# Spreading an attention kernel's PV and q matmuls over column tiles of the PE array

## The chip, the cores and the metric

The kernel runs on one core of a Trainium2 chip. The metric is the time of one execution on the device in microseconds (us). PE is the matmul engine (TensorE), DVE the vector engine, ACT the scalar engine, POOL the general one, SP the engine that issues the loads here. PE has a clock of its own. It is granted at full or at half rate and at nothing between (matmuls of 512 columns in a row start 216 or 427 ns apart); "clock" below means this granted rate, 1.00 being full.

## The reference

Two independent problems, A and B, each one decode step of sliding-window attention; the outputs are concatenated. Cut to what matters:

```python
B, Sq, D = 2, 1, 576;  Hq, Hkv, Sk, Dh = 32, 16, 16384, 128
W = min(4096, max(256, Sk // 4))                 # 4096: only the last W keys count
q = (x @ wq).reshape(B, Sq, Hq, Dh).transpose(0, 2, 1, 3)
k = repeat(k_cache[:, :, Sk - W:, :], 2, axis=1) # two query heads share a kv head
v = repeat(v_cache[:, :, Sk - W:, :], 2, axis=1)
p = softmax(einsum("bhqd,bhkd->bhqk", q, k) * Dh ** -0.5)
o = einsum("bhqk,bhkd->bhqd", p, v)
out = o.transpose(0, 2, 1, 3).reshape(B, Sq, Hq * Dh) @ wo   # all bf16
```

There is one query row per head and 134.2 MB of k and v to read, so arithmetic per byte is small. With wq and wo, 153.1 MB are read.

## The kernel before

The work comes in 32 slabs (16 kv heads of A, then of B), four slabs to a group, eight groups. A slab is 2 MB (2048 KB) of k and as much of v, for both batches. PV is the product of the probabilities and v. The loads go through one DMA queue into a ring of eight 2 MB slots, always in the same order: k of slab t, then v of slab t-5, and once per group a piece of wo.

For each slab DVE transposes k in two halves, and PE computes scores of both query heads and both batches. For each group a softmax chain follows: maximum (DVE), two tiny PE jobs, exponentials (ACT), a transpose of the probabilities (DVE), sums, reciprocals. Then PV. Slab m of a group owns 32 of the 128 PSUM partitions, which is one column tile of the PE array, and its 16 matmuls run one behind the other:

```python
ot = OTB[32 * m:32 * m + 32, :]
for j in range(j0, j1, 4):          # ... j0, j1 = 0, 64; the last slab in two parts
    z, bk, jj = j // 32, (j % 32) // 16, j % 16
    col = 512 * bk + 64 * (4 * z + m) + 4 * jj
    last = e.matmul(ot, pT[:, v, col:col + 32], ring[:, r, j * 128:(j + 4) * 128],
                    start=(j == 0), stop=(j == KR - 4), skip_group_check=True)
```

When all four slabs of a group are done, ACT evicts the bank, four matmuls with a selection matrix collect the wanted rows, DVE multiplies by the reciprocal sums, and eight matmuls, a mask and a reduction lay the heads out for the projection:

```python
evac_op[G] = [S.add("act", lambda e: e.activation(oE[:, :], OTB[:, :], ACTF.Copy), ...)]   # oE is fp32
for c in range(4):
    last = e.matmul(bank[:, 0:16], oE[:, 128 * c:128 * c + 128], selv[:, c, :], ...)
# ... norm (DVE), then
for j in range(8):
    last = e.matmul(bank[:, 16 * j:16 * j + 16], spread[:, j, :], oTg[...], start=True, stop=True)
# ... mask (DVE), reduce (DVE), then 16 projection matmuls into two column tiles
```

The q stage runs 36 matmuls per problem, each into one column tile (the same for all 36) of four different banks.

## Time and profile before

| | before |
|---|---|
| median of the first three executions | 379.18 us (377.11 to 382.23) |
| the traced execution | 382.22 us, of which the trace spans 380.5 us |
| PE busy | 309.3 us, 81% of the span |
| last load landed | 363.7 us after the span's start |
| last PV matmul ended | 372.7 us |

The busy row of the slices on the profile page (40 equal slices of the span, busy share in tenths; PEclk is the granted clock; DMA the busy share of the 16 DMA engines), kernel before:

```profile
PE   0778995998969876995969876797969976996895
PEclk9999898899889998999889988899689989897697
DMA  8999999999999999999999999999999999999900
```

PE looks almost full, but the row that never dips is DMA. It stops two slices before the end. The table by stretches shows where (columns: stretch in us, its length, then busy us and instruction count of PE, PEld (weight loads), DVE, ACT, POOL; then clock, DMA share, GB/s), kernel before:

```profile
350.00:355.00 5.00, 5.00 (x14) 1.84 (x13) 0.86 (x3) 0.00 (x0) 0.00 (x0) 0.55 1.00 427
362.00:364.00 2.00, 2.00 (x22) 1.09 (x22) 0.00 (x0) 0.00 (x0) 0.00 (x0) 1.00 0.11 43
364.00:366.00 2.00, 2.00 (x15) 0.97 (x11) 0.00 (x0) 0.00 (x0) 0.00 (x0) 1.00 0.00 0
```

Nothing moves after 364 us, yet the kernel goes on for 16 us. The trace also holds each landing of a load: most 2 MB slabs land 4.9 us after the one before, the last v slab at 360.3 us, its cut-off end at 360.9, the last two pieces of wo at 363.0 and 363.7.

What PE does in that time is seen in the timeline (start, duration, engine, line, operation, output and inputs, count; times in us), kernel before:

```profile
341.49 3.63 PE L537 MATMUL ot<-ring,pT 128*32 128x512 bf16 x16
349.60 6.05 PE L537 MATMUL ot<-ring,pT 128*32 128x512 bf16 x16
358.38 4.65 PE L537 MATMUL ot<-ring,pT 128*32 128x512 bf16 x14
...
364.35 8.40 PE L537 MATMUL ot<-ring,pT 128*32 128x512 bf16 x46
372.78 0.60 ACT L549 ACTIVATE oE<-ot 128x512 f32<-128x512 f32 x1 [16.10 <-PE ot L537]
373.43 1.06 PE L554 MATMUL tb<-selv,oE 128*128 128x16 f32 x8 [0.69 <-ACT oE L549]
374.53 0.17 DVE L561 TENSOR_TENSOR oTg<-tb,rsb 128x16 bf16<-128x16 f32 x1 [15.44 <-PE tb L554]
374.76 0.36 PE L575 MATMUL tb<-oTg,spread 128*128 128x16 bf16 x8 [0.27 <-DVE oTg L561]
...
375.83 2.08 PE L601 MATMUL pj<-wob,oP 128*2 128x288 bf16 x16 [0.71 <-DVE oP L587]
```

The first line is PV of slab 26 at full clock (3.6 us), the second PV of slab 27 at mostly half clock (6.1 us), and the line with x46 is nearly all of slabs 29 to 31. When the last v piece landed (360.9 us) PE was still in slab 28. So the end of this kernel is a queue of PE work behind loads that are already there.

### The profile page before, as it was taken

The page shows a single profiled execution, that of the slowest core. Times are in us where ns is not written, and L with a number is a line of the kernel's source. Part 1 is how long each engine was busy: PE and PEld are TensorE (multiplying, and loading weights), DVE is VectorE, ACT ScalarE, POOL GpSimd, SP SyncE. Part 2 cuts the span into 40 slices and gives each one's busy share as a digit, 9 for nine tenths or more (in the row PEclk, how much of TensorE's full clock was granted, in tenths as well). Part 3 has the DMA queues.
Part 4 walks back from the last instruction along what each step waited for, and adds up shares of the span by engine and source line. Part 5 has one row for each costly group of instructions (what it writes and reads, how often), then busy time and mean ns, then how long its engine had stood idle before and what let it go on. Part 6 is the DMA issues. An engine that isn't in the chain of part 4 may idle for free.

```text
span 380.5 us, 3541 instructions
## 1 busy us (share of the span) xinstructions
PE 309.3 (81%) x1500; PEld 133.4 (35%) x1500; DVE 184.4 (48%) x191; ACT 30.7 (8%) x104; POOL 15.5 (4%) x50
## 2 busy tenths in 40 slices
PE   0778995998969876995969876797969976996895
PEld 0433432343334333442424333243334423442442
DVE  3006596746464473447474473465475364543001
ACT  1022002001200020002000020001100020002001
POOL 6001000000000000000000000000000000000000
PEclk9999898899889998999889988899689989897697
DMA  8999999999999999999999999999999999999900
GB/s 334 434 414 432 431 427 422 432 427 427 425 424 431 424 429 431 425 429 420 434 424 434 422 425 434 422 429 423 429 432 424 432 427 422 428 431 425 382 19 3
DMA packets 10976, 153.34 MB, mean 403 GB/s; under 512 B 1224, under 2 KB 1232, under 8 KB 1616
## 3 DMA queue, kind: packets, MB, share of 16 engines
q1 hardware_dynamic: 10948, 153.10, 94.9%
q8 instruction: 12, 0.20, 0.2%
q14 instruction: 4, 0.03, 0.0%
q10 hardware_dynamic: 12, 0.01, 0.0%
HBM read 153.10 MB, written 0.00 MB: 402 GB/s over the span
## 4 chain that ended last, share of the span: by engine, by line
PE 51%; DMA 31%; DVE 14%; ACT 2%; issue 2%; DVEq 0%
PE ot L537 20%; DMA ring<-in_B_k_cache_dram 18%; PE st_0 L432 11%; DVE xt L409 11%; PE st_1 L432 10%; DMA ring<-in_A_k_cache_dram 9%; DMA ring<-in_A_wq_dram 4%; PE pj L601 2%; PE st_0 L262 1%; PE tb L554 1%; PE pj L262 1%; PE ot L262 1%; PE st_1 L262 1%; ACT qrow L271 1%; DVE nM L456 1%
## 5 line engine op out<-in xcount | busy, mean ns | idle before, releaser
L409 DVE STREAM_TRANSPOSE xt<-ring 128x2048 f32<-128x2048 f32 x64 | 144.5, 2284 | 88.7 <-DMA ring<-in_A_k_cache_dram 51.0
L432 PE MATMUL st_0<-xt,zq 128*128 128x512 bf16 x256 | 108.4, 424 | 38.1 <-DVE xt L409 38.0
L537 PE MATMUL ot<-ring,pT 128*32 128x512 bf16 x512 | 123.2, 401 | 0.0
L432 PE MATMUL st_1<-xt,zq 128*128 128x512 bf16 x256 | 108.2, 423 | 0.0
L537 PEld LDWEIGHTS ot<-ring,pT 128*32 128x32 bf16 x512 | 48.9, 101 | 73.8 <-issue 26.5
L432 PEld LDWEIGHTS st_0<-xt,zq 128*128 128x128 bf16 x256 | 26.3, 103 | 80.3 <-DVE xt L409 43.9
L432 PEld LDWEIGHTS st_1<-xt,zq 128*128 128x128 bf16 x256 | 26.7, 104 | 31.7 <-issue 10.5
L561 DVE TENSOR_TENSOR oTg<-tb,rsb 128x16 bf16<-128x16 f32 x8 | 1.4, 174 | 47.7 <-PE tb L554 47.7
L396 POOL TENSOR_TENSOR zq<-qs,bmask 128x64 bf16<-128x64 bf16 x32 | 9.2, 292 | 284.5 <-PE st_1 L432 251.2
L475 ACT ACTIVATE bias_sb<-tb 128x2 f32<-128x2 f32 x8 | 1.4, 172 | 228.2 <-PE tb L471 228.2
L601 PE MATMUL pj<-wob,oP 128*2 128x288 bf16 x128 | 14.6, 304 | 0.7 <-DVE oP L587 0.7
L244 PE MATMUL tb<-ident_b,xt 2*128 2x2 bf16 x36 | 2.3, 194 | 10.0 <-DVE xt L214 10.0
L501 DVE STREAM_TRANSPOSE pT<-pR 128x512 bf16<-128x512 bf16 x16 | 10.4, 686 | 0.0
L471 PE MATMUL tb<-ones_f,nMrep 1*128 1x1 f32 x32 | 4.8, 250 | 6.1 <-DVE nMrep L465 6.1
L456 DVE TENSOR_REDUCE nM<-tb 1x8 f32<-1x64 f32 x16 | 2.7, 207 | 14.0 <-PE tb L447 14.0
L262 PE MATMUL st_0<-ring,xU 128*32 128x512 bf16 x18 | 7.8, 434 | 2.1 <-DMA ring<-in_A_wq_dram 2.1
L554 PEld LDWEIGHTS tb<-selv,oE 128*128 128x128 f32 x64 | 8.2, 191 | 2.9 <-ACT oE L549 2.0
L554 PE MATMUL tb<-selv,oE 128*128 128x16 f32 x64 | 7.9, 255 | 1.4 <-ACT oE L549 1.4
L601 PEld LDWEIGHTS pj<-wob,oP 128*2 128x2 bf16 x128 | 6.7, 86 | 4.8 <-DVE oP L587 0.8
L482 ACT ACTIVATE pR<-st_0,bias_sb 128x256 bf16<-128x256 f32 x16 | 8.2, 543 | 0.3
L482 ACT ACTIVATE pR<-st_1,bias_sb 128x256 bf16<-128x256 f32 x16 | 8.2, 550 | 0.0
L441 DVE TENSOR_REDUCE mx<-st_0 128x2 f32<-128x512 f32 x8 | 5.3, 657 | 5.6 <-PE st_1 L432 5.6
(62 smaller groups left out, 109.3 us busy)
## 6 DMA issues: line engine op xcount, KB each, us to landing
ring<-in_A_k_cache_dram SPq DMA_DIRECT2D x16, 2048.0 KB, 32.1
ring<-in_A_v_cache_dram SPq DMA_DIRECT2D x16, 2048.0 KB, 32.8
ring<-in_B_k_cache_dram SPq DMA_DIRECT2D x16, 2048.0 KB, 34.1
ring<-in_B_v_cache_dram SPq DMA_DIRECT2D x15, 2048.0 KB, 29.9
ring<-in_A_wq_dram SPq DMA_DIRECT2D x1, 4608.0 KB, 13.6
ring<-in_B_wq_dram SPq DMA_DIRECT2D x1, 4608.0 KB, 24.1
wob<-in_A_wo_dram SPq DMA_DIRECT2D x4, 1152.0 KB, 26.2
wob<-in_B_wo_dram SPq DMA_DIRECT2D x3, 1152.0 KB, 25.3
```

Of the source, the lines that this page charges most:

```text
L262: last = e.matmul(QB[c][32 * P:32 * P + 32, :], xU[:, P, u, 0:32], wqv[P][:, u, c * 512:(c + 1) * 512], start=(u == 0), stop=(u == NU - 1) ...
L396: return e.tensor_tensor(dst, src, msk, ALU.mult)
L409: Xop[(t, jb)] = S.add("dve", lambda e: e.transpose(xt[:, n % NXT, :].bitcast(FP32), ring[:, r, jb * HW_:(jb + 1) * HW_].bitcast(FP32)), d ...
L432: last = e.matmul(st[bk][:, 0:512], zq[:, p4, m, 16 - 16 * jb:144 - 16 * jb], mv, start=(m == 0 and jb == 0 and p4 == 0), stop=True, skip_ ...
L441: mxs = [S.add("dve", lambda e, jb=jb: e.tensor_reduce(mx[:, jb, :], st[jb][:, :].rearrange("p (x t) -> p t x", t=2), AX.X, ALU.max), [Sop ...
L456: last = e.tensor_reduce(dst, src, AX.X, ALU.max, negate=True)
L471: last = e.matmul(bank[:, t:t + 1], nMrep[0:1, t, :], ones_f[0:1, 0:1], start=True, stop=True)
L482: last = e.activation(pR[:, jb, :].rearrange("p (x t) -> p t x", t=2)[:, t, :], st[jb][:, :].rearrange("p (x t) -> p t x", t=2)[:, t, :], ...
L501: chain[(G, "pT%d" % jb)] = S.add("dve", lambda e, jb=jb: e.transpose(pT[:, v, 512 * jb:512 * jb + 512].rearrange("p (w j q) -> p j w q", ...
L537: last = e.matmul(ot, pT[:, v, col:col + 32], ring[:, r, j * 128:(j + 4) * 128], start=(j == 0), stop=(j == KR - 4), skip_group_check=True)
L554: last = e.matmul(bank[:, 0:16], oE[:, 128 * c:128 * c + 128], selv[:, c, :], start=(c == 0), stop=(c == 3))
L601: last = e.matmul(PJ[half], oP[:, v, j, :], wob[:, v, j, half * NH:(half + 1) * NH], start=(proj_start(G) and j == 0), stop=True, skip_gro ...
```

## The change

The intent: PE work becomes shorter, and the work behind the last PV too.

- PV of a slab is split in its two halves z, which go to two neighbouring column tiles, with the matmuls alternating between them. A slab now fills two column tiles, so the bank holds two slabs and is evicted twice per group. The eviction multiplies by the reciprocal sum as its scale, so the DVE normalisation falls away; for this the reciprocals are written 16 times over, as 256 values.
- The selection sums the two halves, twice four matmul calls for a group; for the last group the first four are issued early, behind PV of slab 29.
- A product with a mask on DVE, two matmuls and an ACT copy replace the eight spread matmuls, the mask and the reduction.
- q of a problem goes to four column tiles of one bank, alternating.

The diff cut to its core:

```diff
-QB = [ST[1][0], ST[1][1], OTB, PJB]
+QB = [OTB, PJB]
-   last = e.matmul(QB[c][32 * P:32 * P + 32, :], xU[:, P, u, 0:32], wqv[P][:, u, c * 512:(c + 1) * 512], ...
+   last = e.matmul(QB[P][32 * c:32 * c + 32, :], xU[:, P, u, 0:32], wqv[P][:, u, c * 512:(c + 1) * 512], ...
...
-chain[(G, "rs")] = ... e.reciprocal(rs[0:1, 0:16], ssum[0:1, 0:16])
+chain[(G, "rs")] = ... e.reciprocal(rsrep[0:1], ssum[0:1, 0:16]. ... .broadcast_to([1, 4, 16, 4]))
...
-ot = OTB[32 * m:32 * m + 32, :]
+js = [32 * z + 4 * k for k in range(8) for z in range(2)]
+   c = 2 * mm + z                                        # mm = m % 2
-   last = e.matmul(ot, pT[:, v, col:col + 32], ring[...], start=(j == 0), stop=(j == KR - 4), ...)
+   last = e.matmul(OTB[32 * c:32 * c + 32, :], pT[:, v, col:col + 32], ring[...],
+                   start=(j % 32 == 0), stop=(j % 32 == 28), ...)
+elif m == 2:
+    deps.append(evac_op[(G, 0)])
...
-S.add("act", lambda e: e.activation(oE[:, :], OTB[:, :], ACTF.Copy), ...)
+S.add("act", lambda e: e.activation(oE[:, pr, :], OTB[:, :], ACTF.Copy, scale=rsb[:, v, pr:pr + 1]), ...)
+for pr in prs:                                            # dg: [0, 1], for the last group [0] early, then [1]
+    for c in range(4):
+        last = e.matmul(bank[:, 0:16], oE[:, pr, 128 * c:128 * c + 128], selv[:, pr, c, :], ...)
...
+last = e.matmul(bank[:, 8 * b:8 * b + 8], oA[:, b].rearrange("d h c -> d (h c)"), jmask[:], start=True, stop=True)
```

More of the change, by code (lines that the diff above doesn't have):

```diff
@@ L109, in build_kernel @@
         sel = sb("sel", [128, 4, 128], BF16)
-        spread = sb("spread", [128, 8, 128], BF16)
         bmask = sb("bmask", [128, 4], FP32)
-        hmask = sb("hmask", [128, 8], FP32)
         mx = sb("mx", [128, 2, 2], FP32)
@@ L120, in build_kernel @@
         ssum = sb("ssum", [1, 16], FP32)
-        rs = sb("rs", [1, 16], FP32)
-        rsb = sb("rsb", [128, 2, 16], FP32)
+        rsrep = sb("rsrep", [1, 4, 16, 4], FP32)
+        rsb = sb("rsb", [128, 2, 2], FP32)
         pR = sb("pR", [128, 2, 512], BF16)
@@ L125, in build_kernel @@
         pT = sb("pT", [128, 2, PW + 16], BF16)
-        oE = sb("oE", [128, 512], FP32)
-        selv = sb("selv", [128, 4, 16], FP32)
-        qrow = sb("qrow", [64, HD // 2], BF16)
-        oTg = sb("oTg", [128, 2, 8, Bb], BF16)
-        oM = sb("oM", [128, 8, 8, Bb], FP32)
+        oE = sb("oE", [128, 2, 512], FP32)
+        selv = sb("selv", [128, 2, 4, 16], FP32)
+        qrow = sb("qrow", [128, NPROB, 512], BF16)
+        cmask = sb("cmask", [128, 16], FP32)
+        jmask_f = sb("jmask_f", [128, 8], FP32)
+        jmask = sb("jmask", [128, 8], BF16)
+        oA = sb("oA", [128, Bb, 8, 16], BF16)
         oP = sb("oP", [128, 2, 8, Bb], BF16)
@@ L194, in build_kernel @@
         p_sel = S.add("pool", f_sel, [p_ones_b], "sel")
-        p_spread = S.add("pool", lambda e: e.tensor_copy(
-            spread[:].rearrange("d j (h c) -> d j h c", h=8),
-            ident_b[:].rearrange("d (c j) -> d j c", j=8).unsqueeze(2).broadcast_to([128, 8, 8, 16])), [p_ident_b], "spread")
         p_ones_f = S.add("pool", lambda e: e.memset(ones_f[:], 1.0), [], "ones_f")
@@ L200, in build_kernel, with f_selv @@
                                                             base=0, channel_multiplier=1), [p_ones_f], "ident_f")
+        p_zsel = S.add("pool", lambda e: e.memset(selv[:].rearrange("p r c k -> p (r c k)"), 0.0), [], "zero_selv")
+        def f_selv(e):
+            for pr in range(2):
+                for mm in range(2):
+                    o = 4 * pr + 2 * mm
+                    dst = selv[:, pr].rearrange("p c (b k) -> p c b k", b=Bb)[:, :, :, o:o + 2]
+                    a0, a1 = (ident_f[:, 64 * mm + 32 * z:64 * mm + 32 * z + 16].rearrange("p (c b h) -> p c b h", c=4, b=Bb) for z in range(2))
+                    last = e.tensor_tensor(dst, a0, a1, ALU.add)
+            return last
+        p_selv = S.add("pool", f_selv, [p_ident_f, p_zsel], "selv")
         p_zq = S.add("pool", lambda e: e.memset(zq[:].rearrange("d p m w -> d (p m w)").bitcast(FP32), 0.0), [], "zero_zq")
         p_zpt = S.add("pool", lambda e: e.memset(pT[:, :, PW:PW + 16], 0.0), [], "zero_pT")
-        p_selv = S.add("pool", lambda e: e.affine_select(
-            selv[:].rearrange("p c (m q) -> p c m q", m=4), ones_f[:, 0:64].rearrange("p (c m q) -> p c m q", c=4, m=4),
-            [[-4, 4], [-32, 4], [-1, 4]], ALU.is_equal, 0.0, base=0, channel_multiplier=1), [p_ones_f], "selv")
         p_off = S.add("pool", lambda e: e.memset(nMrep[:].rearrange("o t r -> o (t r)"), OFF), [], "off")
@@ L218, in build_kernel @@
                      [p_ident_f], "bmask")
-        d_hm = S.add("dve", lambda e: e.tensor_reduce(hmask[:, 0:8], ident_f[:].rearrange("p (h i) -> p h i", h=8), AX.X, ALU.add),
-                     [p_ident_f], "hmask")
+        d_cm = S.add("dve", lambda e: e.tensor_reduce(cmask[:, 0:16], ident_f[:].rearrange("p (c j) -> p c j", j=8), AX.X, ALU.add),
+                     [p_ident_f], "cmask")
+        d_jf = S.add("dve", lambda e: e.tensor_reduce(jmask_f[:, 0:8], ident_f[:].rearrange("p (c j) -> p j c", j=8), AX.X, ALU.add),
+                     [p_ident_f], "jmask_f")
+        d_jm = S.add("dve", lambda e: e.tensor_copy(jmask[:], jmask_f[:]), [d_jf], "jmask")
         tbn = [0]
@@ L253, in build_kernel @@
         qs_ev = {}
-        QB = [ST[1][0], ST[1][1], OTB, PJB]
+        QB = [OTB, PJB]
         NC4 = UW // 512
         assert NC4 == 4
+        q_ev = {}
         for P in range(NPROB):
@@ L261, in f_q @@
                     for c in range(NC4):
-                        last = e.matmul(QB[c][32 * P:32 * P + 32, :], xU[:, P, u, 0:32], wqv[P][:, u, c * 512:(c + 1) * 512],
+                        last = e.matmul(QB[P][32 * c:32 * c + 32, :], xU[:, P, u, 0:32], wqv[P][:, u, c * 512:(c + 1) * 512],
                                         start=(u == 0), stop=(u == NU - 1), skip_group_check=True)
                 return last
-            op = S.add("pe", f_q, [wq_dma[P], op_xev] + ([q_ev] if P else []), "q%d" % P)
+            op = S.add("pe", f_q, [wq_dma[P], op_xev], "q%d" % P)
             q_done[P] = op
-            def f_qe(e, P=P):
-                last = None
-                for c in range(NC4):
-                    last = e.activation(qrow[32 * P:32 * P + 2 * Bb, c * 512:(c + 1) * 512], QB[c][32 * P:32 * P + 2 * Bb, :], ACTF.Copy)
-                return last
-            q_ev = S.add("act", f_qe, [op], "qe%d" % P)
+            q_ev[P] = S.add("act", lambda e, P=P: e.activation(qrow[:, P, :], QB[P][:, :], ACTF.Copy), [op], "qe%d" % P)
             def f_qt(e, bank, P=P):
@@ L277, in f_qt, with f_qte @@
                 bb = bank[:].bitcast(BF16)
-                for cb in range(NCB):
-                    last = e.transpose(bb[0:128, 2 * Bb * cb:2 * Bb * (cb + 1)], qrow[32 * P:32 * P + 2 * Bb, cb * 128:(cb + 1) * 128],
-                                       ident_b[32 * P:32 * P + 2 * Bb, 32 * P:32 * P + 2 * Bb])
-                return last
-            n_, bank, op = tb_job(f_qt, "qt%d" % P, [q_ev])
-            eo = S.add("act", lambda e, bank=bank, P=P: e.activation(
-                qT[:, P, :].rearrange("d (s h b) -> d s h b", s=2, b=Bb),
-                bank[:].bitcast(BF16)[:, 0:NCB * 2 * Bb].rearrange("d (h s b) -> d s h b", s=2, b=Bb), ACTF.Copy), [op], "qte%d" % P)
+                for k in range(4):
+                    last = e.transpose(bb[0:128, 128 * k:128 * k + 128], qrow[:, P, k * 128:(k + 1) * 128], ident_b[:])
+                return last
+            n_, bank, op = tb_job(f_qt, "qt%d" % P, [q_ev[P], p_ident_b])
+            def f_qte(e, bank=bank, P=P):
+                for s in range(2):
+                    last = e.activation(
+                        qT[:, P, :].rearrange("d (s c k b) -> d s c k b", s=2, c=4, b=Bb)[:, s],
+                        bank[:].bitcast(BF16)[:, 0:512].rearrange("d (k c w) -> d c k w", k=4, c=4)[:, :, :, Bb * s:Bb * s + Bb], ACTF.Copy)
+                return last
+            eo = S.add("act", f_qte, [op], "qte%d" % P)
             tb_consumer[n_] = eo
@@ L420, in make_S @@
                 deps.append(exp_op[G - 2])
-            if t == 4:
-                deps.append(q_ev)
             def f(e):
@@ L508, in make_chain2, with f_rb @@
             tb_consumer[n3] = sm
-            chain[(G, "rs")] = S.add("dve", lambda e: e.reciprocal(rs[0:1, 0:16], ssum[0:1, 0:16]), [sm] + prev("rsbm"), "rs%d" % G)
+            chain[(G, "rs")] = S.add("dve", lambda e: e.reciprocal(
+                rsrep[0:1], ssum[0:1, 0:16].rearrange("o (m q) -> o m q", m=4).unsqueeze(2).broadcast_to([1, 4, 16, 4])),
+                [sm] + prev("rsbm"), "rs%d" % G)
         def make_chain3(G):
             v = G % 2
-            n4, b4, rb = tb_job(lambda e, bank: e.matmul(bank[:, 0:16], ones_f[0:1, 0:128], rs[0:1, 0:16], start=True, stop=True),
-                                "rsbm%d" % G, [chain[(G, "rs")], p_ones_f])
+            def f_rb(e, bank):
+                for pr in range(2):
+                    last = e.matmul(bank[:, pr:pr + 1], rsrep[0:1, 2 * pr:2 * pr + 2].rearrange("o m z q -> o (m z q)"), ones_f[0:1, 0:1],
+                                    start=True, stop=True)
+                return last
+            n4, b4, rb = tb_job(f_rb, "rsbm%d" % G, [chain[(G, "rs")], p_ones_f])
             chain[(G, "rsbm")] = rb
@@ L517, in make_chain3 @@
             if G >= 2:
-                deps.append(norm_op[G - 2])
-            rsb_op[G] = S.add("act", lambda e: e.activation(rsb[:, v, :], b4[:, 0:16], ACTF.Copy), deps, "rsb%d" % G)
+                deps.append(evac_op[(G - 2, 1)])
+            rsb_op[G] = S.add("act", lambda e: e.activation(rsb[:, v, 0:2], b4[:, 0:2], ACTF.Copy), deps, "rsb%d" % G)
             tb_consumer[n4] = rsb_op[G]
@@ L526, in make_PV @@
             v = G % 2
-            ot = OTB[32 * m:32 * m + 32, :]
+            mm = m % 2
             parts = [(0, KR, stream_dma[("V", i)])]
@@ L531, in make_PV, with f @@
             for j0, j1, dma in parts:
-                def f(e, j0=j0, j1=j1):
+                js = [32 * z + 4 * k for k in range(8) for z in range(2)]
+                def f(e, js=[j for j in js if j0 <= j < j1]):
                     last = None
-                    for j in range(j0, j1, 4):
+                    for j in js:
                         z, bk, jj = j // 32, (j % 32) // 16, j % 16
+                        c = 2 * mm + z
                         col = 512 * bk + 64 * (4 * z + m) + 4 * jj
-                        last = e.matmul(ot, pT[:, v, col:col + 32], ring[:, r, j * 128:(j + 4) * 128],
-                                        start=(j == 0), stop=(j == KR - 4), skip_group_check=True)
+                        last = e.matmul(OTB[32 * c:32 * c + 32, :], pT[:, v, col:col + 32], ring[:, r, j * 128:(j + 4) * 128],
+                                        start=(j % 32 == 0), stop=(j % 32 == 28), skip_group_check=True)
                     return last
@@ L541, in make_PV, with make_evac @@
                 if m == 0:
-                    deps += evac_op[G - 1] if G >= 1 else [q_ev]
+                    deps += [evac_op[(G - 1, 1)]] if G >= 1 else [q_ev[0]]
+                elif m == 2:
+                    deps.append(evac_op[(G, 0)])
                 PVop[i] = S.add("pe", f, deps, "PV%d_%d" % (i, j0))
             last_reader[("V", i)] = PVop[i]
-        def make_norm(G):
+        def make_evac(G, pr):
             v = G % 2
-            pdep = [PVop[4 * G + 3]] + ([chain[(G - 1, "dg")]] if G >= 1 else [])
-            evac_op[G] = [S.add("act", lambda e: e.activation(oE[:, :], OTB[:, :], ACTF.Copy), pdep, "oE%d" % G)]
-            def f_dg(e, bank):
+            deps = [PVop[4 * G + 2 * pr + 1], rsb_op[G]] + ([chain[(G - 1, "dg")]] if G >= 1 else [])
+            evac_op[(G, pr)] = S.add("act", lambda e: e.activation(oE[:, pr, :], OTB[:, :], ACTF.Copy, scale=rsb[:, v, pr:pr + 1]),
+                                     deps, "oE%d_%d" % (G, pr))
@@ L552, in f_dg, with make_dg, f @@
+        dg_job = {}
+        def make_dg(G, prs):
+            if G not in dg_job:
+                n = tbn[0]
+                tbn[0] += 1
+                dg_job[G] = (n, TB[n % 2])
+                extra = [tb_consumer[n - 2], p_selv]
+            else:
+                extra = []
+            bank = dg_job[G][1]
+            def f(e):
                 last = None
-                for c in range(4):
-                    last = e.matmul(bank[:, 0:16], oE[:, 128 * c:128 * c + 128], selv[:, c, :], start=(c == 0), stop=(c == 3))
@@ L555, in f_dg @@
-                return last
-            n_, bank, op = tb_job(f_dg, "dg%d" % G, evac_op[G] + [p_selv])
-            chain[(G, "dg")] = op
-            deps = [op, rsb_op[G]]
-            if G >= 2:
-                deps.append(proj_op[G - 2])
-            norm_op[G] = S.add("dve", lambda e: e.tensor_tensor(
-                oTg[:, v, :, :].rearrange("d (m h) b -> d m h b", m=4), bank[:, 0:16].rearrange("d (m b h) -> d m h b", b=Bb, h=2),
-                rsb[:, v, 0:16].rearrange("d (m b h) -> d m h b", b=Bb, h=2), ALU.mult), deps, "norm%d" % G)
@@ L564, in make_norm, with make_A @@
-            tb_consumer[n_] = norm_op[G]
+                for pr in prs:
+                    for c in range(4):
+                        last = e.matmul(bank[:, 0:16], oE[:, pr, 128 * c:128 * c + 128], selv[:, pr, c, :],
+                                        start=(pr == 0 and c == 0), stop=(pr == 1 and c == 3))
+                return last
+            chain[(G, "dg")] = S.add("pe", f, [evac_op[(G, pr)] for pr in prs] + extra, "dg%d" % G)
+        def make_A(G):
+            n, bank = dg_job[G]
+            op = S.add("dve", lambda e: e.tensor_tensor(
+                oA[:].rearrange("d b h c -> d (b h) c"), bank[:, 0:16].unsqueeze(2).broadcast_to([128, 16, 16]),
+                cmask[:, 0:16].unsqueeze(1).broadcast_to([128, 16, 16]), ALU.mult),
+                [chain[(G, "dg")], d_cm] + ([chain[(G - 1, "rl")]] if G >= 1 else []), "A%d" % G)
+            tb_consumer[n] = op
+            chain[(G, "A")] = op
@@ new lines, in make_rl, with f @@
+        def make_rl(G):
+            v = G % 2
+            def f(e, bank):
+                for b in range(Bb):
+                    last = e.matmul(bank[:, 8 * b:8 * b + 8], oA[:, b].rearrange("d h c -> d (h c)"), jmask[:], start=True, stop=True)
+                return last
+            n_, bank, op = tb_job(f, "rl%d" % G, [chain[(G, "A")], d_jm])
+            chain[(G, "rl")] = op
+            chain[(G, "oP")] = S.add("act", lambda e: e.activation(
+                oP[:, v, :, :].rearrange("p j b -> p b j"), bank[:, 0:8 * Bb].rearrange("p (b j) -> p b j", b=Bb), ACTF.Copy),
+                [op] + ([proj_op[G - 2]] if G >= 2 else []), "oP%d" % G)
+            tb_consumer[n_] = chain[(G, "oP")]
@@ L566, in proj_start @@
         def proj_start(G):
             return G % GP == 0
-        def make_spread(G):
-            v = G % 2
-            def f_rl(e, bank):
-                last = None
-                for j in range(8):
-                    last = e.matmul(bank[:, 16 * j:16 * j + 16], spread[:, j, :], oTg[:, v, :, :].rearrange("d h b -> d (h b)"),
-                                    start=True, stop=True)
-                return last
-            n_, bank, op = tb_job(f_rl, "rl%d" % G, [norm_op[G], p_spread])
-            mo = S.add("dve", lambda e: e.tensor_tensor(
-                oM[:].rearrange("p j h b -> p j h b"), bank[:, 0:128].rearrange("p (j h b) -> p j h b", j=8, h=8),
-                hmask[:, 0:8].unsqueeze(1).unsqueeze(3).broadcast_to([128, 8, 8, Bb]), ALU.mult),
-                [op, d_hm] + ([chain[(G - 1, "oP")]] if G >= 1 else []), "oM%d" % G)
-            tb_consumer[n_] = mo
-            def f_op(e):
-                with nc.allow_low_precision(reason="one term of the sum is not zero"):
-                    return e.tensor_reduce(oP[:, v, :, :], oM[:].rearrange("p j h b -> p j b h"), AX.X, ALU.add)
-            chain[(G, "oP")] = S.add("dve", f_op,
-                [mo] + ([proj_op[G - 2]] if G >= 2 else []), "oP%d" % G)
@@ L605, in make_proj @@
                 if proj_start(G):
-                    deps += [e_ops[(P - 1, 0)], e_ops[(P - 1, 1)]] if P >= 1 else [q_ev]
+                    deps += [e_ops[(P - 1, 0)], e_ops[(P - 1, 1)]] if P >= 1 else [q_ev[1]]
                 proj_op[G] = S.add("pe", f, deps, "proj%d_%d" % (G, j0))
@@ L629, in build_kernel @@
             if Gp is not None:
-                make_norm(Gp)
-                make_spread(Gp)
+                make_dg(Gp, [1] if Gp == NG - 1 else [0, 1])
             if t < NSLAB:
@@ L636, in build_kernel @@
                     make_Z(t + 4)
+            if Gp is not None:
+                make_A(Gp)
             if Gc is not None:
                 make_chain2(Gc)
+            if Gp is not None:
+                make_rl(Gp)
             if 0 <= i < NSLAB:
@@ L642, in build_kernel @@
                 make_chain3(Gc)
+            if 0 <= i < NSLAB and i % 2 == 1:
+                make_evac(i // 4, (i % 4) // 2)
+                if i == NSLAB - 3:
+                    make_dg(NG - 1, [0])
             if Gp is not None:
```

## The prediction

> **What bounds the kernel now.** The DMA queue, not TensorE, although the page shows PE 81% busy. The slices' DMA row is 9 almost everywhere, at 414 to 434 GB/s. Most landings follow one another by 4.9 us per 2 MB slab from 41 us to 356 us, whatever PE does. The last v slab lands at 360.3 us, its cut-off end at 360.9, the last two pieces of wo at 363.0 and 363.7. The span is 380.5 us: 17 us lie behind the stream. Only they can shrink.
>
> **What fills those 17 us** (timeline). PE arrives late: the scores of the last k slab end at 341.5, 5.5 us after their second transpose; the last softmax chain then leaves PE nearly idle from 345.1 to 349.6; the clock row shows half speed afterwards, so PV of two slabs takes 6.0 and 4.6 us instead of 3.5; the last three slabs run at 216 ns per matmul until 372.7. Then follow serially: eviction, 8 fp32 matmuls, normalise, spread, mask, reduce (3.1 us to the first projection matmul), projection 2.1, output copy and store (4.6 us from the first of these to the end).
>
> **What the change does.** PV's two halves go to different column tiles. The trace already shows such overlap: the two projection halves start 6 ns apart, and where PV passes to the next slab's column tile four matmuls pair up 6 to 16 ns apart; within a slab they are 216 ns apart (427 at half clock). This agrees with the Trainium skill, "TensorE: Matmul & The Clock Gate", Part 3, which says matmuls in different column groups run concurrently (2.38x for three tiles). Estimate: a slab's PV falls from 3.45 to 1.75 us warm, 6.8 to 3.4 cold. q falls from 36 serial matmuls (10.7 us cold, 7.7 warm) to about 4 and 2. Before 337 us this is hidden behind the loads.
> Added: a second 0.6 us eviction per group, which PV must wait for twice per group (about 0.7 us each).
>
> **On the critical path.** Estimate of the new end: scores end near 338, the last chain's gap moves to 340–344, PV then follows the loads and ends about 362 (360.9 plus two matmuls would be the floor; a cold stretch or the eviction wait costs 1 to 2 us). From there to the projection 2.4 instead of 3.1 us (half the selection matmuls are done early; two spread matmuls and an ACT copy replace eight, a mask and a reduction). Then 4 to 4.6 us as before: span about 369. The profiled run's time was 1.7 us over its span: about 370.5 us.
>
> **Predicted: 370.5 us, 80% range 367.5 to 374.5.** Faster by over 2%: 0.67; within: 0.32; slower: 0.01.
>
> **What would show it right.** PV busy about halved, partners starting 6 to 16 ns apart; landings still 4.9 us per slab and ending near 363.7; mean clock lower; last PV end 361.5 to 364 instead of 372.7; 6.2 to 7 us from there to the end.
>
> **What would make it wrong.** Two streams may contend (pairs slower than 216 ns). With less work the clock may stay at half through the tail (same page, Part 1: it follows activity; this trace agrees, half speed in windows of 3.4 us after idle stretches): PV would end near 365 to 367 and the gain fall under 2%. The stream could slow by stragglers among the 16 engines: its last engine already lags 3.5 us behind the first.

## The result, and the profile after

| | before | after |
|---|---|---|
| median | 378.56 us (376.22 to 382.23, 6 executions) | 373.99 us (372.36 to 374.73, 6 executions) |
| traced execution, span | 380.5 us | 370.6 us |
| PE busy | 309.3 us | 262.9 us |
| PV matmuls busy | 123.2 us | 66.7 us |
| mean clock of the traced execution | 0.91 | 0.85 |
| last load landed | 363.7 us | 363.7 us |
| last PV matmul ended | 372.7 us | 363.0 us |

The ratio of the times is 0.9886 (95% interval 0.9847 to 0.9925): 1.1% faster, inside the predicted range, but not over the 2% that the prediction thought likeliest. (A ratio is the mean time of one kernel's fast runs over that of the other's of the same rounds, so not quite the ratio of the medians quoted here. An execution over 1.5% above the fastest of the same kernel counts as slow. Among these six the traced execution, of 382.2 us, is 1.6% above the fastest, and 0.9886 is the ratio without it; the other five have a median of 378.26 us. So the rows of the table that come from the traces set a slow execution against a fast one and overstate the change; the medians hardly do. The run b_again below is a second trace of the kernel before.)

The slices, kernel after:

```profile
PE   0626975875788747857788758785789467778685
PEclk9965998898599899988699698988599698988887
DMA  8999999999999999999999999999999999999990
```

The DMA row is as full as before and now ends one slice before the end of the span. The shares by engine in the chain of work that ended last, first before, then after:

```profile
PE 51%; DMA 31%; DVE 14%; ACT 2%; issue 2%; DVEq 0%
```

```profile
DMA 80%; PE 7%; DVE 6%; issue 4%; ACT 1%; SPq 0%
```

The chain moved from PE to the loads. The groups of instructions that the change touched (line, engine, operation, output and inputs, shapes, count, then busy us and mean ns, then idle time before), kernel before:

```profile
L537 PE MATMUL ot<-ring,pT 128*32 128x512 bf16 x512 | 123.2, 401 | 0.0
L554 PE MATMUL tb<-selv,oE 128*128 128x16 f32 x64 | 7.9, 255 | 1.4 <-ACT oE L549 1.4
L509 DVE RECIPROCAL rs<-ssum 1x16 f32<-1x16 f32 x8 | 1.9, 241 | 0.3
```

and after:

```profile
L550 PE MATMUL ot<-ring,pT 128*32 128x512 bf16 x512 | 66.7, 412 | 0.0
L583 PE MATMUL tb<-selv,oE 128*128 128x16 f32 x128 | 15.2, 259 | 2.4 <-ACT oE L564 2.4
L513 DVE RECIPROCAL rsrep<-ssum 1x256 f32<-1x256 f32 x8 | 13.9, 1741 | 0.3
```

PV has the same 512 matmuls of the same mean length, but as two run side by side its busy time is almost halved. Two lines went the other way: the selection matmuls doubled from 64 to 128 records, and the reciprocal over 256 values takes 1.74 us instead of 0.24. The timeline of the end, kernel after:

```profile
345.41 3.59 PE L550 MATMUL ot<-ring,pT 128*32 128x512 bf16 x16
350.37 1.96 PE L583 MATMUL tb<-selv,oE 128*128 128x16 f32 x16 [0.84 <-ACT oE L564]
352.99 3.21 PE L550 MATMUL ot<-ring,pT 128*32 128x512 bf16 x16
...
356.98 1.46 PE L550 MATMUL ot<-ring,pT 128*32 128x512 bf16 x12
358.48 0.69 ACT L564 ACTIVATE oE<-ot,rsb 128x512 f32<-128x512 f32 x1 [5.19 <-PE ot L550]
359.22 1.06 PE L583 MATMUL tb<-selv,oE 128*128 128x16 f32 x8 [0.78 <-ACT oE L564]
360.22 2.79 PE L550 MATMUL ot<-ring,pT 128*32 128x512 bf16 x32
363.08 0.69 ACT L564 ACTIVATE oE<-ot,rsb 128x512 f32<-128x512 f32 x1 [3.91 <-PE ot L550]
363.82 1.06 PE L583 MATMUL tb<-selv,oE 128*128 128x16 f32 x8 [0.82 <-ACT oE L564]
...
365.89 2.08 PE L624 MATMUL pj<-wob,oP 128*2 128x288 bf16 x16 [0.28 <-ACT oP L606]
```

Slabs 30 and 31 together take 2.79 us. But PV pauses for 4.0 us between slab 27 (ends 349.0) and slab 28, where before it was 2.7 us (355.65 to 358.38), and for 1.8 us between slabs 29 and 30, where before there was nothing. In these pauses PE waits for an eviction and runs the selection. And from the last PV to the projection it is 2.9 us (363.0 to 365.9), where it was 3.1.

### The profile page after: what moved, and what is told of

Read it like the earlier page. It is cut to its first block, busy times and chain, and to the rows that moved or that the text cites. A ratio compares the mean times of both kernels' runs of the same rounds, so it can differ in the third digit from the quotient of the medians.

```text
span 370.6 us, 3564 instructions
## 1 busy us (share of the span) xinstructions
PE 262.9 (71%) x1508; PEld 114.9 (31%) x1508; DVE 194.6 (53%) x177; ACT 35.7 (10%) x116; POOL 14.2 (4%) x53
## 4 chain that ended last, share of the span: by engine, by line
DMA 80%; PE 7%; DVE 6%; issue 4%; ACT 1%; SPq 0%
DMA ring<-in_B_k_cache_dram 41%; DMA ring<-in_A_k_cache_dram 39%; DVE xt L415 6%; PE ot L550 3%; PE tb L583 1%; PE pj L624 1%; PE st_0 L436 1%; PE st_1 L436 1%; ACT pR L486 1%; ACT oE L564 1%; DVE oA L590 0%; SPq L177 0%; SPq L370 0%; PE tb L475 0%; PE tb L521 0%
## 5 line engine op out<-in xcount | busy, mean ns | idle before, releaser
L436 PE MATMUL st_0<-xt,zq 128*128 128x512 bf16 x256 | 115.2, 450 | 70.0 <-DVE xt L415 70.0
L436 PE MATMUL st_1<-xt,zq 128*128 128x512 bf16 x256 | 115.2, 450 | 0.0
L550 PE MATMUL ot<-ring,pT 128*32 128x512 bf16 x512 | 66.7, 412 | 0.0
L550 PEld LDWEIGHTS ot<-ring,pT 128*32 128x32 bf16 x512 | 24.2, 103 | 36.9 <-issue 18.0
L564 ACT ACTIVATE oE<-ot,rsb 128x512 f32<-128x512 f32 x16 | 11.0, 685 | 78.5 <-PE ot L550 78.5
L583 PE MATMUL tb<-selv,oE 128*128 128x16 f32 x128 | 15.2, 259 | 2.4 <-ACT oE L564 2.4
L583 PEld LDWEIGHTS tb<-selv,oE 128*128 128x128 f32 x128 | 15.4, 191 | 4.4 <-ACT oE L564 3.5
L590 DVE TENSOR_TENSOR oA<-tb,cmask 128x256 bf16<-128x256 f32 x8 | 3.4, 425 | 25.3 <-PE tb L583 25.3
L513 DVE RECIPROCAL rsrep<-ssum 1x256 f32<-1x256 f32 x8 | 13.9, 1741 | 0.3
L624 PE MATMUL pj<-wob,oP 128*2 128x288 bf16 x128 | 10.1, 305 | 0.3 <-ACT oP L606 0.3
L271 PE MATMUL pj<-ring,xU 128*32 128x512 bf16 x36 | 4.0, 631 | 5.6 <-DMA ring<-in_B_wq_dram 5.6
```

Source lines behind the costliest of these rows:

```text
L271: last = e.matmul(QB[P][32 * c:32 * c + 32, :], xU[:, P, u, 0:32], wqv[P][:, u, c * 512:(c + 1) * 512], start=(u == 0), stop=(u == NU - 1) ...
L436: last = e.matmul(st[bk][:, 0:512], zq[:, p4, m, 16 - 16 * jb:144 - 16 * jb], mv, start=(m == 0 and jb == 0 and p4 == 0), stop=True, skip_ ...
L513: chain[(G, "rs")] = S.add("dve", lambda e: e.reciprocal(rsrep[0:1], ssum[0:1, 0:16].rearrange("o (m q) -> o m q", m=4).unsqueeze(2).broad ...
L550: last = e.matmul(OTB[32 * c:32 * c + 32, :], pT[:, v, col:col + 32], ring[:, r, j * 128:(j + 4) * 128], start=(j % 32 == 0), stop=(j % 32 ...
L564: evac_op[(G, pr)] = S.add("act", lambda e: e.activation(oE[:, pr, :], OTB[:, :], ACTF.Copy, scale=rsb[:, v, pr:pr + 1]), deps, "oE%d_%d" ...
L583: last = e.matmul(bank[:, 0:16], oE[:, pr, 128 * c:128 * c + 128], selv[:, pr, c, :], start=(pr == 0 and c == 0), stop=(pr == 1 and c == 3))
```

## The experiments

Twelve runs followed, two repeats and ten edited kernels, in four jobs on different chips, each beside executions of the kernel before. Differences within a job are safer than differences of medians between jobs.

### Both kernels again

No edit. Why do two traces differ by 9.9 us of span while the medians differ by 4.6 us?

> The changed kernel unaltered, for a second trace. Question: why is the gain 4.6 us by the medians (378.56 to 373.99) when the two traces differ by 9.9 us of span (380.5 to 370.6)? Theory A (tail clock): the load stream ends at 363.7 us in every execution; the executions differ in which 3.4 us windows of the last 20 us run at half clock, so PV's end and the steps after it move. Expect last landing 363.7 +- 0.3 and a span of 370.5 to 373 explained by PV and projection. Theory B (stream): executions differ because the stream ends 1 to 3 us earlier or later; expect the last landing to move with the span and the time from the last landing to the end to stay 6.9 us.

> The kernel before unaltered, for a second trace; its first trace was of one of its slowest executions (382.2 against a median of 378.6). Theory A: last landing again 363.7 +- 0.3, span near 377, and the 3 to 4 us less are found between 345 and 373 us, as slabs of PV at 3.5 us that took 6.0 and 4.6 in the first trace. Theory B: last landing near 360, same tail.

Measured: the changed kernel 374.11 us (372.65 to 374.79), ratio 0.9884 (0.9798 to 0.9969), last landing 363.8; the kernel before 378.05 us in its second trace, span 376.3, last landing 364.0. In the same job seven executions of the kernel before spread from 376.62 to 382.41 us, the two over 382 us counted as slow and are in no ratio. (The first trace was of an execution of 382.2 us, which by the same rule is slow among the six of the result. The second is 0.4% above the fastest of its job.) The kernel before, second trace, in the stretches and lines that were shown of the first:

```profile
350.00:355.00 5.00, 4.24 (x20) 2.14 (x18) 0.00 (x0) 0.67 (x2) 0.00 (x0) 0.83 1.01 431
```

```profile
347.85 5.31 PE L537 MATMUL ot<-ring,pT 128*32 128x512 bf16 x16
355.87 3.19 PE L537 MATMUL ot<-ring,pT 128*32 128x512 bf16 x14
...
360.38 8.40 PE L537 MATMUL ot<-ring,pT 128*32 128x512 bf16 x46
```

Theory A holds for the stream, but the clock explains only part of what it was to explain. The stream ended within 0.3 us in both traces of this kernel, and the x46 block takes the same 8.40 us, but it starts 4.0 us earlier: 1.8 us of that were there already when PV of slab 27 started (347.85 instead of 349.60), 0.7 us in slab 27 and 1.5 us in slab 28, which ran at full clock this time (with the projection matmuls behind it). So 2.2 us of the 4.0 lie in the two slabs whose clock differed and 1.8 us in how late PE already was. The first trace was of one of the slowest executions; comparing it with one of the fastest of the changed kernel overstates the gain.

### PV without the alternation

```diff
-js = [32 * z + 4 * k for k in range(8) for z in range(2)]
+js = [32 * z + 4 * k for z in range(2) for k in range(8)]
```

> The changed kernel with PV's matmuls in the order of the kernel before: eight in one column tile, then eight in the other; everything else stays. If the alternation is what pays (my theory), PV of a slab takes 3.5 us again, the end of PV moves from 363.0 to about 371 to 373 us, and the time is 377 to 383 us, the two added evictions making it no better than before. Rival: the gain came from the shorter chain behind PV and the smaller q stage; then the time stays within 1 us of 374.

Measured: 378.82 us (377.18 to 379.36), ratio to before 1.0004 (0.9935 to 1.0073); PV busy 93.4 us; last PV ended at 370.9 us, last landing 363.9. The group of its PV matmuls:

```profile
L550 PE MATMUL ot<-ring,pT 128*32 128x512 bf16 x512 | 93.4, 397 | 0.0
```

With everything else of the change in place and only the order of the 16 matmuls put back, the gain is gone. The shorter layout chain and the q stage do not pay for the added evictions and selections; the alternation is what pays. (PV busy did not return to 123 us, as there are now two places per slab where the column tile changes and a few matmuls overlap.)

### q without the alternation

```diff
-for u in range(NU):
-    for c in range(NC4):
+for c in range(NC4):
+    for u in range(NU):
```

> The changed kernel with the q matmuls running through one column tile after the other (nine each), so that only the boundaries overlap. q then takes about 8 to 10 us again instead of 4. My theory: hidden behind the loads, the time stays within 0.7 us of the changed kernel's, the landings do not move. Rival: q sets when ring slots come free and so when the stream runs; then landings come later by up to 6 us and the time with them.

Measured: 373.53 us (372.81 to 374.17), ratio to before 0.9871, against 0.9884 for the changed kernel in the same job. The first and the last matmul of q0 started at 14.5 and 21.4 us instead of 14.9 and 18.0; the third load of the trace (k of slab 0) landed at 31.42 instead of 31.49 us. The q part of the change gives nothing that these runs can see: it is hidden behind loads.

### The early selection moved behind the last PV

```diff
+if i == NSLAB - 1:
+    make_dg(NG - 1, [0])          # right behind PV of the last slab
-if i == NSLAB - 3:
-    make_dg(NG - 1, [0])
```

> The changed kernel with the early half of the last group's selection matmuls moved behind the last PV, so that PE runs them while ACT evicts. In the two traces of the changed kernel PE stands 1.8 us between the PV of slabs 29 and 30 (eviction 0.7, selection 1.06). Theory 1 (PE order costs in the tail): the gap shrinks to 0.8 us, PV ends 0.8 to 1.1 us earlier (near 362 to 363.3, not under 361.4, where the last load lets it), and since the moved matmuls cost 0.2 to 0.4 us more behind the eviction the time falls by 0.5 to 0.9 us, to about 373.2. Rival (the landings bind PV already): time within 0.3 us of the changed kernel.

Measured: 372.54 us (371.66 to 373.11), ratio 0.9861 (0.9838 to 0.9883). The wait between slabs 29 and 30 fell from 1.8 to 0.9 us, as expected; PV of this trace still ended at 363.95, because slabs 28 and 29 ran at half clock until 359.1. By the medians of two jobs 1.4 us were won, by the ratios (0.9861 against 0.9886) 0.9 us: as expected or a little more. The intervals of the ratios overlap, and in this trace the projection ran at full clock (1.14 us; 2.08 in both traces of the changed kernel), so that the order on PE costs time is likely but not separated from the clock.

### Three edits together

dg_late, the reciprocal on 16 values followed by a DVE copy that broadcasts them (0.24 and 0.28 us), and the bf16 edit that is shown further down.

> As dg_late, and selection matmuls in bf16 (one pass each instead of two), and the reciprocal on 16 values followed by a broadcast copy (instead of a 1.74 us reciprocal over 256). By theory 1 the selection of group 6 falls from 1.96 to about 0.5 us on PE between PV 27 and 28, and the last selection from 1.06 to about 0.3, so PV ends at 361.5 to 363 and the projection starts 2.2 us later instead of 2.9: time 371.5 to 372.5, 1.5 to 2.5 us less than the changed kernel. Rival (landings bind): only the 0.7 us behind PV.

Measured: 370.25 us (369.95 to 370.33), ratio 0.9801 (0.9781 to 0.9821). The last PV ended at 362.4, the projection began 2.1 us later. This was more than expected, and the spread of five executions was 0.4 us. dg_late ran in the same job, so the 2.3 us between the two (372.54 and 370.25) are those of the other two edits.

### The kernel before, kept at full clock in the last chain

```diff
+def fill(n, deps, tag):      # matmuls into a PSUM bank that nobody reads any more
+    def f(e):
+        for _ in range(n):
+            last = e.matmul(ST[0][0][:, 0:512], ident_b[:], xt[:, 1, 0:512], start=True, stop=True, ...)
+        return last
+    S.add("pe", f, deps + [exp_op[NG - 2], Xop[(NSLAB - 2, 1)]], tag)
 # in the last group only: 3 behind the maxima's transposes, 9 behind the bias, 3 behind the reciprocals' broadcast
```

> The kernel before with 15 idle-filling matmuls into an unused PSUM bank, in the three waits of the last softmax chain. If the clock of the tail makes the executions differ (376.2 to 382.4 us) and made the first trace 2 us slower than the median, then full clock from 345 to 373 us should bring every execution to 375 to 377 us with a spread under 2 us; PV of slab 27 takes 3.5 us. Rival: the clock is a symptom only, median stays near 379.

Measured: 376.30 us (374.06 to 377.52), ratio 0.9955 (0.9921 to 0.999). In its trace the clock is full from the softmax chain to 370.5 us and PV of slab 27 takes 3.63 us instead of 6.05, as expected. The median is 1.5 us below that of the eleven executions of the kernel before in the job (377.77), but the spread stayed at 3.5 us, so that expectation failed: the clock of the last 30 us is one cause of the differences between executions and not the only one. How far PE lags before 340 us is another by the traces (the last scores ended at 341.6, 339.9 and 340.9 us in the three traces of this kernel); it was not tested by itself.

### Half of PV left out

```diff
-js = [32 * z + 4 * k for k in range(8) for z in range(2)]
+js = [32 * z + 4 * k for k in (0, 2, 4, 7) for z in range(2)]
```

> Wrong on purpose: the changed kernel with half of PV's matmuls left out. It asks what a still faster PV could give. Estimate: PV of a slab 0.9 us instead of 1.75 (warm); if the loads and the chain set the end, PV ends at 361.4 to 362 instead of 363 to 364.3 and the time is 372 to 372.7, at most 2 us less. If PE time still sets the tail, five slabs save 5 to 8 us and the time falls under 370.

Measured: 370.92 us (370.19 to 372.10), a wrong result. The last PV ended at 361.3, 0.5 us behind the landing of the last piece of v (360.86). Half of the PV work away is worth 3.1 us against the median of the changed kernel in another job (I expected at most 2), although five slabs at 0.9 us less each (an estimate from the 1.9 us of a slab at full clock) would make 4 to 5 us of PE time in the tail alone. In the same job tail_all, with all of PV, is faster (370.25). This suggests that what is left to gain lies less in PV than in what stands between its slabs. In this trace PE also waits 0.95 us for the reciprocal, whose 1.74 us end after PV of slab 27.

### Selection in bf16, alone

```diff
-oE = sb("oE", [128, 2, 512], FP32)
-selv = sb("selv", [128, 2, 4, 16], FP32)
+oE = sb("oE", [128, 2, 512], BF16)
+selv = sb("selv", [128, 2, 4, 16], BF16)
```

> The changed kernel with the evicted rows and the selection matrix in bf16, nothing else; it asks which of the three edits of tail_all (370.25 us) paid. fp32 selection runs as two passes: 16 matmul records of 112 ns between PV of slabs 27 and 28, 8 behind the last PV. If doubling the selection work is what ate the expected shorter chain, bf16 gives 0.4 us and 0.3 us for these, PV ends 1 to 2 us earlier and the chain from PV's end to the projection is 2.1 instead of 2.9 us: time 371.2 to 372.2. Rival (the reciprocal over 256 values paid, by releasing the eviction earlier): then only 0.7 us of the 3.7 us of tail_all, time 373.2.

Measured: 370.17 us (369.92 to 370.60), ratio 0.9773 (0.9735 to 0.9812), correct. That is all of what the three edits gave together, and 1 us more than expected. (The ratio differs from theirs because the executions of the kernel before were slower in this job, with a mean of 378.6 us instead of 377.7.) The group of the selection matmuls and the end of the timeline, this kernel:

```profile
L583 PE MATMUL tb<-selv,oE 128*128 128x16 bf16 x64 | 3.0, 170 | 2.5 <-ACT oE L564 2.5
```

```profile
350.17 0.36 PE L583 MATMUL tb<-selv,oE 128*128 128x16 bf16 x8 [0.84 <-ACT oE L564]
...
357.95 1.90 PE L550 MATMUL ot<-ring,pT 128*32 128x512 bf16 x16
360.26 1.90 PE L550 MATMUL ot<-ring,pT 128*32 128x512 bf16 x16 [0.40 <-DMA ring<-in_B_v_cache_dram]
362.24 0.69 ACT L564 ACTIVATE oE<-ot,rsb 128x512 bf16<-128x512 f32 x1 [4.53 <-PE ot L550]
362.98 0.26 PE L583 MATMUL tb<-selv,oE 128*128 128x16 bf16 x4 [0.82 <-ACT oE L564]
...
364.24 1.15 PE L624 MATMUL pj<-wob,oP 128*2 128x288 bf16 x16 [0.28 <-ACT oP L606]
```

Half the records, each a fraction as long: 8 in 0.36 us where 16 took 1.96. The second to last PV line is new in kind: PV of slab 31 now waits for its load ("<-DMA"), which PE in the tail of neither kernel did. The projection takes 1.15 us instead of 2.08, because it ends just before the clock falls (at 365.5). Against the two traces of the changed kernel this one is 2.6 and 3.9 us shorter: PV ends 0.8 and 2.1 us earlier, the way to the projection is 0.8 us shorter, and 0.9 us are the clock of the projection, which no expectation had. The reciprocal over 256 values is still in this kernel: its 1.74 us ended at 348.2, before PV of slab 27 did (348.8), so there it kept nobody waiting.

### The changed kernel with filled waits, and tail_all with filled waits

The same fill as above in the changed kernel; in tail_all with further fills (2 behind the selection of each of the last two groups, 2 behind the last early selection, 1 behind the last spread).

> The changed kernel with the same 15 idle-filling matmuls in the waits of the last softmax chain. In its traces PV of slabs 27 and 28 took 3.4 us at half clock instead of 1.9. If half clock in the tail is what keeps it 2 to 3 us above the estimate, PV 27 and 28 run at full clock, PV ends at 361.5 to 362.5, and the time is 371.5 to 372.5. If the clock falls back right after (PE has too little work), the time stays at 373 to 374.

> tail_all plus the filling matmuls, here also in the waits of the last two groups' spread and of the last eviction. tail_all's PV 27 to 29 ran at half clock and ended at 362.4, 1 us above what the loads allow (361.4). Expect PV's end at 361.4 to 361.8 and 369.2 to 370.0 us, 0.3 to 1.0 less than tail_all; if fillers get in the way of the chain, 370.3 or more.

Measured: 372.76 us (372.03 to 372.86) and 371.25 us (370.01 to 371.56). The first is about 1.2 us below the changed kernel in another job. PV of slab 27 took 1.9 us instead of 3.6, but then PE waited 1.0 us for the reciprocal over 256 values (it ended at 348.5, PV of slab 27 at 347.5), slabs 28 and 29 were at half clock again, and PV ended at 364.2 us, not at 361.5 to 362.5: that expectation failed. Beside the second trace of the changed kernel, where PV ended at 364.3, the 1.0 us that this trace is shorter lies in the projection (1.14 us at full clock instead of 2.08). The second kernel is 1.0 us worse than the same one without fills, which ran in another job, and 1.1 us worse than dg_bf16 in its own job: a miss. Its trace shows why. Stretches of tail_all with fills:

```profile
350.00:355.00 5.00, 4.93 (x60) 2.27 (x58) 0.42 (x1) 0.19 (x1) 0.00 (x0) 1.00 0.99 418
355.00:360.00 5.00, 1.93 (x18) 0.72 (x16) 0.00 (x0) 0.69 (x1) 0.00 (x0) 1.00 0.98 403
360.00:362.00 2.00, 1.67 (x8) 0.58 (x10) 0.00 (x0) 0.00 (x0) 0.00 (x0) 0.55 0.53 216
```

```profile
360.33 3.50 PE L565 MATMUL ot<-ring,pT 128*32 128x512 bf16 x16 [2.44 <-DMA ring<-in_B_v_cache_dram]
```

Being early, PE stood idle for 2.4 us before the last slab's load, and the clock was at half just when that slab came: 3.50 us instead of 1.90. To be early helped nothing here; that the idle time brought the half clock fits this trace and was not tested by itself. The six executions fall in two heaps (370.0 and 371.0 to 371.6), which would fit a window of the clock that falls one way or the other; only one of them was traced.

### The last slab in three pieces

dg_bf16, with v of the last slab loaded in pieces of 1/2, 3/8 and 1/8, each with columns of both halves:

```diff
-v_cut = KR - 8                                           # 7/8, then 1/8
+vcuts = [(0, 4, None), (4, 7, mid_sem), (7, 8, last_sem)]  # in units of one matmul of each half
+for z in range(2):
+    last = e.dma_start(d0[:, z, k0 * 512:k1 * 512], s0[:, :, z, k0 * 512:k1 * 512]).then_inc(sm, 16)
```

> dg_bf16 with the last v slab loaded in three pieces (1/2, 3/8, 1/8, each with columns of both halves, so that the matmul pairs stay) instead of 7/8 and 1/8. In dg_bf16's trace PV of slab 31 starts only when 7/8 of it have landed (360.26 us) and ends at 362.16, 1.2 us behind the last piece (near 360.9). If that landing is what binds now, half of PV 31 runs before 360.3, PV ends at 361.4 to 361.6, and the time is 369.3 to 369.9, 0.3 to 0.8 us less than dg_bf16 (370.17). Rival: smaller packets or six more transfers delay the stream's end, and the time is 370.2 or more.

Measured: 369.56 us (368.94 to 369.81), ratio 0.9771 (0.9732 to 0.9811), correct. Its median is the lowest of all that ran. The last piece of v landed at 361.2 us and PV ended at 361.6, 0.6 us earlier than in the trace of dg_bf16; the last piece of wo landed at 364.0 and the projection ended at 364.8. So the trace fits the expectation that the landing of the large piece had bound. The 0.6 us to dg_bf16 in the medians are less certain: it ran in another job, the two ranges do not overlap, but the ratios to the kernel before are the same (0.9771 and 0.9773).

## Why the prediction was right or wrong

- **The bound: right.** The loads were the floor in every trace taken (last landing 363.6 to 364.0 us in all fourteen), whatever PE did. Only the time behind them moved.
- **The alternation: right, in kind and size.** Partners start 1 to 5 ns apart in the trace of the changed kernel, pairs follow one another at 215 to 226 ns at full clock (median 216) and mostly at 427 at half, so a slab's matmuls start within 1.7 us (8 pairs) instead of 3.45 (16 times 216 ns). Two streams did not get in each other's way. Without that order the gain is gone (378.82 us). This agrees with the Trainium skill, "TensorE: Matmul & The Clock Gate", Part 3, which says that matmuls in different column groups of the array run at the same time.
- **q hidden behind the loads: right** (373.53 us without it).
- **The tail behind PV: wrong, and this is the step that failed.** The prediction put 2.4 us from the last PV to the projection because "half the selection matmuls are done early". The trace of the changed kernel has 2.9 us, as the other half is as much as all of it was before: the change doubled the calls (two evictions per group), and fp32 makes two records of each call, which the x8 of the kernel before for four calls already showed. The same doubling put 1.96 us instead of 1.06 between PV of slabs 27 and 28 and 1.06 us between slabs 29 and 30, so PE fell behind the loads again and PV ended at 363.0, 364.3 and 365.4 us in the three traces with the alternation, this selection order and no fills (the third with q serial), not at "about 362". With the selection in bf16 and nothing else changed, PV ended at 362.2, the projection began 2.1 us later, and the time was 370.17 us, where 370.5 had been predicted. This shows that the selection's length is what the sum lacked. It does not price the doubling alone, as bf16 takes away more than the doubling brought (0.36 us instead of 1.96 between slabs 27 and 28, where the kernel before had 1.06), and 0.9 us of the gain came by way of the projection's clock. That 370.17 meets 370.5 so closely is in part luck.
- **The eviction wait (0.7 us, twice per group): right in size.** In the tail it is the 0.8 us before each selection line; dg_late shows it as a 0.9 us wait when nothing is added to it.
- **The clock: foreseen as a risk, and in part it came.** PV of slabs 27 and 28 ran mostly at half clock (3.6 and 3.2 us), and the mean clock fell from 0.91 to 0.85. By medians, filling the waits gave 1.2 us, and in before_warm the same fill gave 1.5 us.
- **The chance of over 2%: too high.** The estimate of 370.5 us lay only 0.3% under that line, so 0.5 us more behind PV and 1 to 3 us more before its end were enough to cross it. The median of the kernel before was no sure mark either: its fast executions ranged over 5 us.
- **Not foreseen, and mostly hidden:** the reciprocal over 256 values, 1.74 instead of 0.24 us, 13.9 us of DVE in all. In the tails of the changed kernel and of dg_bf16 it ended before PV of slab 27 did. Where that PV was made shorter, PE waited for it: 1.0 us in after_warm and in pv_half. Its price was not tried alone.

## What to carry to other kernels

When loads are the floor, price a change by what lies behind the last landing, and count there every call that the change adds, with the record count that the trace shows for that kind of call: here the selection, doubled and in fp32, kept back 3.8 of the 8.4 us that the same change brings with a selection in bf16 (medians 378.56 before, 373.99 changed, 370.17 with bf16; the last is of another job, and in its trace 0.9 us is the clock of the projection). Where small matmuls use few columns, let neighbours in time go to different column tiles; here the order of issue was enough to have the gain or not. And do not compare single traces of a kernel whose tail depends on a clock that changes in windows: look at the spread first.

## What the Trainium skill lacked or had wrong

- "FP8 and Floating Point Precision", section "TensorE Precision Notes", says that true fp32 takes four passes through the array. The trace shows two matmul records per fp32 call here (64 records for 8 groups of 4 calls), 112 ns apart with 16 columns, and one of bf16, 25 ns apart. How many passes a record stands for is not shown; where expectations above speak of passes, records were counted. The page gives no time for narrow fp32 matmuls: four calls took 1.06 us, the same in bf16 0.26 us.
- "TensorE: Matmul & The Clock Gate", Part 1, says that the throttle's window of 3.4 us is free-running and so varies between runs. These traces agree: half clock came in stretches of 3.4 us and multiples of it up to 17.1 us, and the first edge of the window grid lay anywhere from 0.1 to 3.4 us after the start of the span. The under 1% that the page allows for modelling is for the ramp at the start of a kernel; what a half-rate window costs depends on where it falls. Here two traces of the kernel before, whose load streams ended within 0.3 us, are 4.2 us apart, 2.2 us of it in the PV of two slabs whose clock differed, and the last projection took 1.15 us at full clock and 2.08 at half.
- The same page, Part 3, gives 2.38x for three column tiles. For two tiles, which it does not list, this case has 2.0x within a slab (16 matmuls at 216 ns against 8 pairs at 216 ns).
- The same page, section "LDWEIGHTS", puts a weight load at columns / 1.2 ns, which makes an estimate of about 27 ns for 32 columns. The records of PV's 32-column loads are mostly 92 to 97 ns at full clock, no less than those of the 128-column bf16 loads of the scores (median 95 to 96 ns); "TensorEngine Tiling (Array Packing)", "Restrictions", says that column tiling switches the fast weight load off, but no run here tells what causes this.
- "VectorE: DVE Perf Modes", section "First, the fixed hardware budget", says that the reciprocal is an iterative divide and gives no time. Here 16 values on one partition took 241 ns and 256 took 1741 ns, 6.25 ns for each further value; a copy of 256 took 280 ns.
